# Gate logits of an attention and mixture-of-experts kernel: one pass per batch, added up in PSUM and turned on VectorE

## The chip, the cores and the metric

The kernel runs on one core of a Trainium2 chip. The metric is device time in microseconds of one execution, the median of several runs. The names of the engines are those of the profile: PE is TensorE's matmul, PEld its weight load, DVE is VectorE, ACT is ScalarE, POOL is GpSimd, SP is SyncE, whose queue carries most of the large transfers. SBUF is the on-chip memory, PSUM the eight banks of 512 float32 columns into which PE writes.

## What is computed

Eight batches of 448 tokens with 12 heads of 64 go through attention with a sigmoid in place of the softmax. The 768 values of each token then go through two gates and, by the larger logit, to one of 8 experts.

```python
scores = scale * np.matmul(q, k.transpose(0, 1, 3, 2)) - np.log(S)
attn_out = np.matmul(1.0 / (1.0 + np.exp(-scores)), v)
x = attn_out.transpose(0, 2, 1, 3).reshape(B * S, H * D)
logits = x @ w_gate                       # (3584, 8)
e_idx = np.argmax(logits, axis=1)
gate_w = softmax(logits)[np.arange(N), e_idx]
eom = 1.0 / (1.0 + np.exp(-(x @ w_output_gate)))
out[mask] = gate_w[mask, None] * eom[mask, e, None] * (np.maximum(x[mask] @ w1[e], 0.0) @ w2[e])
```

The last line runs for each expert e, with `mask = e_idx == e`.

## The kernel before

**Attention.** The 96 heads are 48 pairs, six pairs a batch. `attention` walks through 24 groups of two pairs in 7 units each, 168 units and two more, since the values run two units behind the scores. In each unit PE does four score matmuls (line 810) and four value matmuls (line 819), each of four in its own 64 by 64 corner of the array, and ACT one sigmoid over 896 columns (line 812). After units 3 and 6 of a group the function `evict` has DVE add the two halves of a pair's output from PSUM into an SBUF tile `x` (128 channels by 448 tokens, line 832), turn it in blocks of 32 (line 833) and, after a batch's last pair, has SP write the batch to DRAM as rows (line 835).

**Gates.** `wg` holds both gates' weights for each pair, 128 by 32, of which 16 columns are used. `gates(k)` runs in unit 3 of every second group, and once more after attention: four pairs' tiles `x` are multiplied with their weights at once, each pair in its own 32 columns of the array (line 849), so that each pair's part of the logits lands in its own 32 partitions of PSUM bank 6. DVE copies or adds these parts to a tile `gl` in SBUF (lines 856, 858, 859, 861). A batch has six pairs, so a call can end one batch and begin the next.

**Route.** `route(b)` is a generator in five pieces, one for each batch. The piece behind "logits" has PE turn `gl` in four chunks of 112 tokens (line 277, into bank 5, or bank 7 after attention), so that tokens lie on partitions; DVE adds the four 32-row parts (line 278) and finds the largest logit (lines 281 to 285, up to `oh`, a 0/1 mark). Behind "counts" PE counts marks with `tri` and `ones` (lines 293 to 299) and ACT takes sigmoids. Behind "places" ACT copies the counts and POOL works out each token's place in its expert's list (lines 303 to 313). Behind "rows" POOL writes each token's record into the lists in DRAM with four indirect DMAs (line 319). In attention the pieces run in units 5, 0, 1 and 3; the last batch's run in `side()` between steps of the first expert tile.

**Experts.** `slot(m)` takes 256 tokens of one expert. POOL gathers their rows (line 504), DVE turns them, ACT and DVE split rows and weights into a high and a low part (lines 538 to 545), PE does layer 1 (lines 582 and 583) and layer 2 (lines 607 to 609). Layer 1's sums go through three tiles that lie in the same memory as `gl`. The first slots take tokens of batches 0 to 5, so that the expert stage starts without the last batches.

**Order.** The program is recorded in the order in which it is written, engine by engine; no scheduler moves anything. Each engine runs its own instructions in that order.

## Time and profile before

| what | us |
|---|---|
| median of 3 runs (779.05 to 780.46) | 779.47 |
| the profiled execution, its own time | 779.45 |
| its span, first to last instruction | 777.74 |
| PE busy in the span | 765.6 |
| DVE busy | 498.2 |
| ACT busy | 488.1 |
| POOL busy | 354.6 |
| granted PE clock, share of full | 0.999 |

The span is what the rows below divide up; the 1.7 us between span and time lie around the program. Matmuls are pipelined: the length of one in a row includes its way through the array, so what one costs in a stream is read from the distance of starts. A float32 matmul stands in the trace as two records, each with a weight load of its own: line 849 has 48 matmuls and 96 records.

### The profile page before, as it was taken

The page shows a single profiled execution, that of the slowest core. Times are in us where ns is not written, and L with a number is a line of the kernel's source. Part 1 is how long each engine was busy: PE and PEld are TensorE (multiplying, and loading weights), DVE is VectorE, ACT ScalarE, POOL GpSimd, SP SyncE. Part 2 cuts the span into 40 slices and gives each one's busy share as a digit, 9 for nine tenths or more (in the row PEclk, how much of TensorE's full clock was granted, in tenths as well). Part 3 has the DMA queues.
Part 4 walks back from the last instruction along what each step waited for, and adds up shares of the span by engine and source line. Part 5 has one row for each costly group of instructions (what it writes and reads, how often), then busy time and mean ns, then how long its engine had stood idle before and what let it go on. Part 6 is the DMA issues. An engine that isn't in the chain of part 4 may idle for free. (4 is left out here: it accounts for less than half of the span.)

```text
span 777.7 us, 15123 instructions
## 1 busy us (share of the span) xinstructions
PE 765.6 (98%) x5724; PEld 559.8 (72%) x5724; DVE 498.2 (64%) x804; ACT 488.1 (63%) x662; POOL 354.6 (46%) x464
## 2 busy tenths in 40 slices
PE   9999999999999999999999999999999999999996
PEld 4333433333433369899999979999998999889785
DVE  3344444443455768977786577668576685977887
ACT  5666666666667757466574565657475574665686
POOL 4003301230331677778885676263462724524622
PEclk9999999999999999999999999999999999999999
DMA  7352544445258560147566487620146856387692
GB/s 262 136 214 98 190 161 174 165 144 214 72 215 297 180 202 16 42 152 257 214 239 244 164 309 265 223 72 31 51 150 220 300 174 214 124 329 252 227 409 65
DMA packets 37615, 145.20 MB, mean 187 GB/s; under 512 B 5639, under 2 KB 7791, under 8 KB 33552
## 3 DMA queue, kind: packets, MB, share of 16 engines
q1 hardware_dynamic: 27696, 119.56, 43.1%
q0 software_dynamic: 9824, 24.46, 9.4%
q8 instruction: 49, 0.80, 0.4%
q14 instruction: 46, 0.38, 0.1%
HBM read 152.61 MB, written 23.05 MB: 226 GB/s over the span
## 5 line engine op out<-in xcount | busy, mean ns | idle before, releaser
L812 ACT ACTIVATE a<-ps,bias_s 128x896 f32<-128x896 f32 x168 | 169.1, 1008 | 95.8 <-PE ps L810 95.8
L582 PE MATMUL ps<-rounded 128*128 128x512 f32 (+1 forms) x672 | 226.5, 386 | 1.3 <-PEq L1006 1.0
L504 POOL DMA_INDIRECT plain<-x_dram,lxs x122 | 182.1, 1493 | 65.2 <-issue 39.3
L583 PE MATMUL ps<-rounded 128*128 128x256 f32 (+1 forms) x672 | 184.1, 274 | 1.4 <-DVE due L617 1.2
L810 PE MATMUL ps<-kqv 64*64 64x448 f32 x1344 | 157.8, 540 | 0.4 <-ACT a L812 0.4
L819 PE MATMUL ps<-a,kqv 64*64 64x448 f32 x1344 | 156.6, 536 | 0.0
L607 PE MATMUL ps<-w2h,h 128*128 128x384 f32 x432 | 144.8, 335 | 0.0
L609 PE MATMUL ps<-w2h,h 128*128 128x384 f32 x432 | 144.4, 334 | 0.0
L608 PE MATMUL ps<-w2l,h 128*128 128x384 f32 x432 | 144.3, 334 | 0.0
L582 PEld LDWEIGHTS ps<-rounded 128*128 128x128 f32 x672 | 125.9, 187 | 25.4 <-issue 2.7
L539 DVE TENSOR_TENSOR w2l<-plain,w2h 128x1536 fp32r<-128x1536 f32 x60 | 105.2, 1757 | 58.7 <-ACT w2h L538 58.0
L583 PEld LDWEIGHTS ps<-rounded 128*128 128x128 f32 x672 | 127.2, 189 | 2.0 <-DVE rounded L545 2.0
L819 PEld LDWEIGHTS ps<-a,kqv 64*64 64x64 f32 x1344 | 51.6, 133 | 75.1 <-issue 74.2
L545 DVE TENSOR_TENSOR rounded<-plain,rounded 128x2048 fp32r<-128x2048 f32 x46 | 103.3, 2285 | 2.0 <-ACT rounded L542 2.0
L810 PEld LDWEIGHTS ps<-kqv 64*64 64x64 f32 x1344 | 48.6, 133 | 73.8 <-issue 60.4
L590 ACT COPY gl<-ps 128x256 f32<-128x256 f32 (+1 forms) x112 | 40.3, 360 | 93.2 <-PE ps L583 87.2
L538 ACT CAST w2h<-plain 128x1536 fp32r<-128x1536 f32 x60 | 88.2, 1473 | 16.2 <-PE ps L849 4.4
L542 ACT CAST rounded<-plain 128x2048 fp32r<-128x2048 f32 x46 | 87.3, 1903 | 0.0
L607 PEld LDWEIGHTS ps<-w2h,h 128*128 128x128 f32 x432 | 81.1, 188 | 2.3 <-issue 1.8
L608 PEld LDWEIGHTS ps<-w2l,h 128*128 128x128 f32 x432 | 81.1, 188 | 0.1
L609 PEld LDWEIGHTS ps<-w2h,h 128*128 128x128 f32 x432 | 81.1, 188 | 0.0
L303 POOL TENSOR_TENSOR pos<-pc,off 112x32 f32<-112x32 f32 x8 | 3.8, 474 | 146.2 <-ACT pc L301 146.2
(211 smaller groups left out, 728.7 us busy)
## 6 DMA issues: line engine op xcount, KB each, us to landing
plain<-w SPq DMA_DIRECT2D x68, 768.0 KB
plain<-w SPq DMA_DIRECT2D x48, 1024.0 KB
kqv<-kqv SPq DMA_DIRECT2D x23, 1344.0 KB
x_dram<-xt SPq DMA_DIRECT2D x8, 1344.0 KB
plain<-w SPq DMA_DIRECT2D x6, 512.0 KB
plain<-x_dram,lxs POOLq DMA_INDIRECT x122, 4.2
kqv<-kqv SPq DMA_DIRECT2D x1, 896.0 KB
lst<-plain POOLq DMA_DIRECT2D x1, 726.0 KB, 8.7
```

Source lines behind the costliest of these rows:

```text
L504: self.nc.gpsimd.indirect_dma_start(out=s["xg"][:, g], out_offset=None, in_=x4, in_offset=bass.IndirectOffsetOnAxis(ap=s["lx"][:, g:g + 1] ...
L538: self.nc.scalar.copy(hi, raw)
L539: self.nc.vector.tensor_tensor(lo, raw, r32(hi), ALU.subtract)
L545: self.nc.vector.tensor_tensor(self.w1p[1][k], self.w1r[:, 2 * k:2 * k + 2], r32(self.w1p[0][k]), ALU.subtract)
L582: nc.tensor.matmul(out, wh[d][:, c], both, start=(d == 0), stop=False)
L583: nc.tensor.matmul(ps[:, 0:n], wl[d][:, c], self.xc[:, d, 0, 0:n], start=False, stop=(d == 5))
L607: nc.tensor.matmul(ps, hh[:, f, tk], wh, start=(f == 0), stop=False)
L608: nc.tensor.matmul(ps, hh[:, f, tk], wl, start=False, stop=False)
L609: nc.tensor.matmul(ps, hl[:, f, tk], wh, start=False, stop=(f == 7))
L810: nc.tensor.matmul(ps[half[h], j, 0:S], kg[half[j], e, 0, o:o + 64], kg[half[j], e, 1], start=True, stop=True)
L812: nc.scalar.activation(at[u % 4], ps[:, :, 0:S], AF.Sigmoid, bias=self.bias_s, scale=1.0 / math.sqrt(D))
L819: nc.tensor.matmul(self.ps_o[e][h][half[j], 0:S], v[half[h], 6 if i == 3 else 3 * e + c, j], a[half[h], j], start=(i in ((0, 3 if h else 4 ...
```

## The change

`gates(b)` now runs once for each batch, in unit 3 of every third group and once after attention. All six pairs of a batch are kept in six tiles (two of them the tiles that were `gl`). Each pair's 448 tokens are cut into quarters of 128, 128, 128 and 64; the quarters take the four column groups of the array, and the six pairs add up in PSUM: 24 matmuls of 128 or 64 columns in one call where there were four of 448. The logits then stand in bank 6 whole, 32 rows for each quarter, and DVE turns them from PSUM into SBUF in blocks of 32 with two instructions (the fourth quarter has only two blocks). The copies and adds into `gl`, the four PE transposes and the sum over parts go away. Partitions now hold 128 tokens in two chunks and 96 in two, in place of four times 112; the constants, the marks and the scatter to the lists follow. The piece behind "logits" runs directly behind the gates. Batches 0, 2, 4 and 6 are routed a group earlier; only the "rows" of batch 6 stay where they were.

```diff
+        self.gp = ps[:, 6, 0:QT]
...
-        self.tok = cp.tile([CP, 2, NCH], I32, name="tok")
-        nc.gpsimd.iota(self.tok[:, 0], pattern=[[CP, NCH]], base=0, channel_multiplier=1)
-        nc.gpsimd.iota(self.meta[:, :, :, 4], pattern=[[S, B], [CP, NCH]], base=0, channel_multiplier=1,
-                       allow_small_or_imprecise_dtypes=True)
+        self.tok = cp.tile([128, 2, NCH], I32, name="tok")
+        for q in range(4):
+            r = slice(32 * q, 32 * q + 32)
+            nc.gpsimd.iota(self.tok[r, 0], pattern=[[32, NCH]], base=QT * q, channel_multiplier=1)
+            nc.gpsimd.iota(self.meta[r, :, :, 4], pattern=[[S, B], [32, NCH]], base=QT * q, channel_multiplier=1,
+                           allow_small_or_imprecise_dtypes=True)
...
+        self.spans = [(128, slice(0, 2)), (96, slice(2, 4))]
...
+        for n in ("lg", "oh"):
+            self.nc.gpsimd.memset(self.R[n], 0.0)
...
         yield "logits"
-        ps = self.mm_ps
-        for c in range(NCH):
-            nc.tensor.transpose(ps[0:CP, 128 * c:128 * c + 128], self.gl[b % 2][:, c * CP:(c + 1) * CP], self.ident)
-        v.tensor_reduce(R["lg"], ps[0:CP, 0:128 * NCH].rearrange("p (c e x) -> p c x e", c=NCH, e=4)[:, :, 0:16, :],
-                        AX.X, ALU.add)
+        for n, c in self.spans:
+            v.transpose(R["lg"][0:n, c].rearrange("p c x -> p (c x)"), self.gp[0:n, 32 * c.start:32 * c.stop])
...
-        v.tensor_tensor(R["oh"], R["rk"], bc(R["mf"][:, 1]), ALU.is_equal)
+        for n, c in self.spans:
+            v.tensor_tensor(R["oh"][0:n, c], R["rk"][0:n, c], bc(R["mf"][:, 1])[0:n, c], ALU.is_equal)
...
-        xts = [t(f"x{i}", [128, S]) for i in range(4)]
+        xts = self.gl + [t(f"x{i}", [128, S]) for i in range(4)]
...
-        def gates(k):
-            v, gp = nc.vector, self.ps_o[1][0]
-            for e in range(4):
-                nc.tensor.matmul(gp[32 * e:32 * e + 32, 0:S], self.wg[:, (4 * k + e) % NPAIR], xts[e],
-                                 start=True, stop=True)
-            for b in sorted({(4 * k + e) // NPAIR for e in range(4)}):
-                es = [e for e in range(4) if (4 * k + e) // NPAIR == b]
-                r = slice(32 * es[0], 32 * es[-1] + 32)
-                gl, src = self.gl[b % 2], gp[r, 0:S]
...
+        def gates(b):
+            for p in range(NPAIR):
+                for q in range(4):
+                    n = min(QT, S - QT * q)
+                    nc.tensor.matmul(self.gp[32 * q:32 * q + 32, 0:n], self.wg[:, p], xts[p][:, QT * q:QT * q + n],
+                                     start=(p == 0), stop=(p == NPAIR - 1))
+            routes.append(self.route(b))
+            want[0] = next(routes[0])
...
-            if i == 3 and g and g % 2 == 0:
-                gates(g // 2 - 1)
+            if i == 3 and g and g % 3 == 0:
+                gates(g // 3 - 1)
+                routing("logits")
...
-            for r, name in ((5, "logits"), (0, "counts"), (3, "rows")):
-                if i == r:
+            for r, name in ((0, "counts"), (3, "rows")):
+                if i == r and (name != "rows" or g != NG - 2):
                     routing(name)
         self.layer1_mm(0)
-        gates(NG // 2 - 1)
+        gates(B - 1)
```

**Where instructions stand.** In the program before, PE has around the second call of the gates and the first batch's transposes (names are output and input; `kqv` and `a` are attention's operands, `x` a pair's tile):

```order
L819 MATMUL ps<-a_145,kqv_142 64x448 x4
L849 MATMUL ps<-x_148,wg 32x448
L849 MATMUL ps<-x_149,wg 32x448
L849 MATMUL ps<-x_150,wg 32x448
L849 MATMUL ps<-x_151,wg 32x448
L810 MATMUL ps<-kqv_142 64x448 x4
L819 MATMUL ps<-a_146,kqv_142 64x448 x4
L810 MATMUL ps<-kqv_142 64x448 x4
L819 MATMUL ps<-a_147,kqv_142 64x448 x4
L277 MATMUL ps<-ident,gl_104 112x128 x4
L810 MATMUL ps<-kqv_142 64x448 x4
```

In the changed program, PE has for the whole of the first batch's logits (line 855 is the gates', `gl` now a pair's tile too):

```order
L855 MATMUL ps<-gl_110,wg 32x128 x3
L855 MATMUL ps<-gl_110,wg 32x64
L855 MATMUL ps<-gl_111,wg 32x128 x3
L855 MATMUL ps<-gl_111,wg 32x64
L855 MATMUL ps<-x_156,wg 32x128 x3
L855 MATMUL ps<-x_156,wg 32x64
L855 MATMUL ps<-x_157,wg 32x128 x3
L855 MATMUL ps<-x_157,wg 32x64
L855 MATMUL ps<-x_158,wg 32x128 x3
L855 MATMUL ps<-x_158,wg 32x64
L855 MATMUL ps<-x_159,wg 32x128 x3
L855 MATMUL ps<-x_159,wg 32x64
```

Two calls of four long matmuls and one set of transposes became one run of 24 short matmuls, behind a value matmul and ahead of a score matmul as before.

DVE, before, from the last call of the gates into the first expert slot (L539 are low parts of weights, L591 and L596 layer 1's sums and their low parts, L278 to L285 the last batch's logits):

```order
L858 TENSOR_TENSOR gl_105<-gl_105,ps 64x448
L859 COPY gl_105<-ps 64x448
L539 TENSOR_TENSOR w2l_2460<-plain,w2h 128x1536
L591 TENSOR_TENSOR gl_104<-gl_104,ps 128x256 x2
L596 SCALAR_TENSOR_TENSOR h_2458<-gl_104,h_2457 128x256
L539 TENSOR_TENSOR w2l_2460<-plain,w2h 128x1536
L278 TENSOR_REDUCE lg<-ps 112x64
L281 TENSOR_REDUCE mf<-lg 112x4
L282 TENSOR_TENSOR df<-lg,mf 112x32
L283 SCALAR_TENSOR_TENSOR rk<-df,rev 112x32
L284 TENSOR_REDUCE mf<-rk 112x4
L285 TENSOR_TENSOR oh<-rk,mf 112x32
```

The same place in the changed program (L544, L596 and L601 are the lines that were 539, 591 and 596):

```order
L544 TENSOR_TENSOR w2l_2578<-plain,w2h 128x1536
L596 TENSOR_TENSOR gl_110<-gl_110,ps 128x256 x2
L601 SCALAR_TENSOR_TENSOR h_2576<-gl_110,h_2575 128x256
L544 TENSOR_TENSOR w2l_2578<-plain,w2h 128x1536
L282 STREAM_TRANSPOSE lg<-ps 128x64
L282 STREAM_TRANSPOSE lg<-ps 96x64
L284 TENSOR_REDUCE mf<-lg 128x4
L285 TENSOR_TENSOR df<-lg,mf 128x32
L286 SCALAR_TENSOR_TENSOR rk<-df,rev 128x32
L287 TENSOR_REDUCE mf<-rk 128x4
L289 TENSOR_TENSOR oh<-rk,mf 128x16
L289 TENSOR_TENSOR oh<-rk,mf 96x16
```

The two passes over `gl` are gone from the front, two transposes stand where the sum stood, and the mark takes two instructions.

## Rows read from the trace of the kernel before

**Rows 1.** The page: the span, and busy time of each engine.
```profile
span 777.7 us, 15123 instructions
PE 765.6 (98%) x5724; PEld 559.8 (72%) x5724; DVE 498.2 (64%) x804; ACT 488.1 (63%) x662; POOL 354.6 (46%) x464
```

**Rows 2.** Busy time by stretch: from:to, length, each engine, clock, DMA.
```profile
5.00:278.00 273.00, 272.62 (x2855) 106.42 (x2857) 129.58 (x277) 178.44 (x205) 69.44 (x193) 1.00 0.51 181
278.00:745.00 467.00, 463.58 (x2718) 426.16 (x2714) 340.72 (x502) 284.23 (x427) 271.26 (x242) 1.00 0.54 188
```

**Rows 3.** Timeline of PE around one gates call: start, length, line, count.
```profile
50.50 0.93 PE L810 MATMUL ps<-kqv 64*64 64x448 f32 x8
...
52.00 0.93 PE L810 MATMUL ps<-kqv 64*64 64x448 f32 x8
...
53.61 0.96 PE L849 MATMUL ps<-x,wg 128*32 128x448 f32 x8
54.50 0.98 PE L810 MATMUL ps<-kqv 64*64 64x448 f32 x8
...
56.06 0.93 PE L810 MATMUL ps<-kqv 64*64 64x448 f32 x8
56.81 0.93 PE L819 MATMUL ps<-a,kqv 64*64 64x448 f32 x8
57.67 0.65 PE L277 MATMUL ps<-ident,gl 128*112 128x128 f32 x4
...
59.80 0.93 PE L810 MATMUL ps<-kqv 64*64 64x448 f32 x8
```

**Rows 4.** Line 849 alone: lengths in ns, least, median, most; a window in its first set.
```profile
L849 PE MATMUL ps<-x,wg x96: 539/551/563, 31.5 to 281.7; 128*32 128x448 f32 x96
...
31.52 0.58 PE L849 MATMUL ps<-x,wg 128*32 128x448 f32 x4
```

**Rows 5.** Line 277 alone: lengths in ns, and what ended idle time before it.
```profile
L277 PEld LDWEIGHTS ps<-ident,gl x32: 131/133/135, 57.7 to 284.6; 128*112 128x112 f32 x32
L277 PE MATMUL ps<-ident,gl x32: 272/273/323, 57.7 to 284.7; 128*112 128x128 f32 x32
...
  DVE xh L822: 4.2, 6
```

**Rows 6.** Timeline of PE: the last gates call, transposes and counts, in the first slot.
```profile
281.06 0.28 PE L583 MATMUL ps<-rounded 128*128 128x256 f32 x1
281.27 0.96 PE L849 MATMUL ps<-x,wg 128*32 128x448 f32 x8
282.16 0.50 PE L582 MATMUL ps<-rounded 128*128 128x512 f32 x1
...
284.24 0.28 PE L583 MATMUL ps<-rounded 128*128 128x256 f32 x1
284.36 0.60 PE L277 MATMUL ps<-ident,gl 128*112 128x128 f32 x4
284.71 0.48 PE L582 MATMUL ps<-rounded 128*128 128x512 f32 x1
...
291.15 0.19 PE L293 MATMUL ps<-oh,tri 112*128 112x32 bf16 x1
...
291.26 0.24 PE L299 MATMUL ps<-oh,ones 112*128 112x8 bf16 x4
```

**Rows 7.** Timeline of ACT and DVE at the same place.
```profile
282.34 1.48 ACT L538 CAST w2h<-plain 128x1536 fp32r<-128x1536 f32 x1 [4.43 <-PE ps L849]
...
287.81 1.76 DVE L539 TENSOR_TENSOR w2l<-plain,w2h 128x1536 fp32r<-128x1536 f32 x1 [0.95 <-ACT w2h L538]
289.49 0.42 DVE L278 TENSOR_REDUCE lg<-ps 112x64 f32<-112x256 f32 x1
...
290.90 0.19 DVE L285 TENSOR_TENSOR oh<-rk,mf 112x32 bf16<-112x32 f32 x1
```

**Rows 8.** Groups up to 345 us: busy us, mean ns; idle before, releaser.
```profile
L833 DVE STREAM_TRANSPOSE xt<-x 128x448 f32<-128x448 f32 x48 | 31.0, 645 | 1.6
L856 DVE COPY gl<-ps 128x448 f32<-128x448 f32 (+1 forms) x8 | 5.0, 626 | 7.8 <-PE ps L849 7.7
```

**Rows 9.** Timeline of PE late: the longest stall of the expert stage.
```profile
452.20 0.39 PE L583 MATMUL ps<-rounded 128*128 128x256 f32 x1 [1.24 <-DVE due L617]
```

More of the change, by code (lines that the diff above doesn't have):

```diff
@@ L26 @@
 NT = B * S
-CP = 112
-NCH = S // CP
+NCH = 4
+QT = 32 * NCH
 Q4 = DM // 4
@@ L106, in memory @@
         self.tmp_early = o + 4096
-        self.step = c(o + 8192, B, 4, dt=F32, parts=CP)
-        self.tokf = c(o + 8192 + 16 * B, NCH, 4, dt=F32, parts=CP)
+        self.step = c(o + 8192, B, 4, dt=F32)
+        self.tokf = c(o + 8192 + 16 * B, NCH, 4, dt=F32)
     def late_memory(self):
@@ L153, in constants @@
         nc.gpsimd.dma_start(self.wg[:, :, 0:16], self.wgo)
-        self.ones = cp.tile([CP, 128], BF16, name="ones")
+        self.ones = cp.tile([128, 128], BF16, name="ones")
         nc.gpsimd.memset(self.ones, 1.0)
-        self.tri = cp.tile([CP, 128], BF16, name="tri")
+        self.tri = cp.tile([128, 128], BF16, name="tri")
         nc.gpsimd.memset(self.tri, 1.0)
@@ L161, in constants @@
             t, pattern=pattern, base=base, channel_multiplier=0, allow_small_or_imprecise_dtypes=True)
-        self.rev = cp.tile([CP, E], F32, name="rev")
+        self.rev = cp.tile([128, E], F32, name="rev")
         iota(self.rev, [[-1, E]], E)
@@ L302, in route @@
         v.reciprocal(sg[:, 1], sg[:, 1])
-        tt(R["pos"], R["pc"][0:CP, 0:NCH * E].rearrange("p (c e) -> p c e", e=E),
-           self.off[0:CP].unsqueeze(1).broadcast_to([CP, NCH, E]), ALU.add)
+        tt(R["pos"], R["pc"][:, 0:NCH * E].rearrange("p (c e) -> p c e", e=E),
+           self.off.unsqueeze(1).broadcast_to([128, NCH, E]), ALU.add)
         tt(R["pos"], R["pos"], oh, ALU.mult)
@@ L318, in route @@
         for c in range(NCH):
+            n = self.spans[c // 2][0]
             g.indirect_dma_start(
-                out=self.lst, out_offset=bass.IndirectOffsetOnAxis(ap=R["posi"][:, c:c + 1], axis=0),
-                in_=meta[:, c, :], in_offset=None)
+                out=self.lst, out_offset=bass.IndirectOffsetOnAxis(ap=R["posi"][0:n, c:c + 1], axis=0),
+                in_=meta[0:n, c, :], in_offset=None)
             if b == B - 2:
@@ L830, in evict @@
             b, hp = divmod(m, NPAIR)
-            x, o = xts[m % 4], xt[b % 2]
+            x, o = xts[hp], xt[b % 2]
             nc.vector.tensor_tensor(x, xh, self.ps_o[m % 2][0][:, 0:S], ALU.add)
@@ L844, in routing @@
                     routes.pop(0)
-        def gates(k):
-            v, gp = nc.vector, self.ps_o[1][0]
-            for e in range(4):
-                nc.tensor.matmul(gp[32 * e:32 * e + 32, 0:S], self.wg[:, (4 * k + e) % NPAIR], xts[e],
-                                 start=True, stop=True)
-            for b in sorted({(4 * k + e) // NPAIR for e in range(4)}):
-                es = [e for e in range(4) if (4 * k + e) // NPAIR == b]
-                r = slice(32 * es[0], 32 * es[-1] + 32)
-                gl, src = self.gl[b % 2], gp[r, 0:S]
-                if b % 2 == 0 and k % 3 == 0 or b % 2 and k % 3 == 1:
-                    v.tensor_copy(gl[r], src)
-                elif b % 2 and k % 3 == 2:
-                    v.tensor_tensor(gl[64:128], gl[64:128], src[64:128], ALU.add)
-                    v.tensor_copy(gl[0:64], src[0:64])
-                else:
-                    v.tensor_tensor(gl[r], gl[r], src, ALU.add)
-            for e in range(4):
-                if (4 * k + e) % NPAIR == NPAIR - 1:
-                    routes.append(self.route((4 * k + e) // NPAIR))
-                    if len(routes) == 1:
-                        want[0] = next(routes[0])
+        def gates(b):
[6 more added lines that the diff above has]
+            want[0] = next(routes[0])
         warm = self.rounded[:, 0:256]
```

24 lines of the change are left out of this document (12 added, 12 removed).

## The prediction

> **What bounds the kernel now.** I read the page's busy shares first: PE is busy 98% of the span, no other engine above 64% [rows 1]. A mean over stages can hide a stage with another limit, so the stretches come next: in attention, 5 to 278 us, PE is busy 272.6 of 273.0 us, DVE 129.6, ACT 178.4 and POOL 69.4; in the expert stage up to 745 us PE is busy 463.6 of 467.0 [rows 2]. Busy is not yet "at its peak", so the third view is the timeline of PE. In a plain stretch score groups start at 50.50 and 52.00, one unit of 1.50 us with two groups of 0.75 [rows 3]. Anything that lengthens the distance between these starts is paid in full, since PE waits for nobody; anything that only makes DVE, ACT or POOL lighter is worth nothing in itself. So the sum below is one of PE time, and DVE enters only where PE waits for it.
>
> **What goes from PE in attention.** With a gates call between them, the score groups at 52.00 and 56.06 lie 4.06 us apart where two units take 3.00 [rows 3]: a call costs 1.06. Of this 0.75 is the call's columns (four matmuls side by side, as many columns as one group of attention); the other 0.31 is the entry into another shape of tile, the first weight load and the way back. Transposes cost 0.74: 56.06 to 59.80 is 3.74 [rows 3]. The table of waits says that the transposes waited for DVE's copy `xh`, 4.2 us over six times [rows 5]. I do not count that as a wait. The distance from the value group at 56.81 to the transposes at 57.67 is 0.86, 0.11 more than 0.75, and the way into the gates call costs about as much without such a wait. So no credit beyond 0.74 is due. Before, 11 calls and 7 sets of transposes lie in attention: 11 x 1.06 + 7 x 0.74 = 16.8 us.
>
> **What comes to PE.** Seven calls in attention, each with 24 matmuls of which every one is two records: 12 sets of four, each set as long as its longest, 128 columns. The switch is the same 0.31. What does a set cost? The old call shows that four column groups run at once: four records start within a window in which one takes 563 ns and all four take 0.58 us [rows 4]. No row has sets of 128 columns in this shape. The nearest is the transposes, 128 float32 columns each with a weight load of its own: four in the first slot take 0.60 us, one takes 0.273, so starts lie (0.60 - 0.27) / 3 = 0.11 apart [rows 5, 6], although each load is recorded as 131 to 135 ns. Their loads, of 112 columns, hide under the matmul before; the new ones have four times 32, so I take 0.11. Bound below: a set can hardly cost less than its share of the columns, 0.75 / 2 / 448 x 128 = 0.107. Bound above: each set pays the weight load that the first set of an old call shows, 563 - 539 = 24 ns [rows 4], so 0.134. A call is then 0.31 + 12 x 0.11 = 1.63 (1.59 to 1.92), seven are 11.4. Attention gains 16.8 - 11.4 = **5.4 us**.
>
> Here a rule of the Trainium skill speaks against the change. "TensorE: Matmul & The Clock Gate", section "Part 3: Packing small matmuls", says that a weight load overlaps running matmuls only where its row group differs; all four quarters use all rows. By that rule the upper bound holds, attention gains 3.3 us and the time would come out near 777.1. The rows speak the other way: in the old call only one set shows the 24 ns and the other is at 539 [rows 4].
>
> **DVE in attention.** It loses the passes over `gl`, 626 ns for a typical one [rows 8], and the sum over parts, and gets two transposes from PSUM. No row has these: 128 x 448 takes 645 ns [rows 8], so between that and nothing; by length I take about 0.25 each, as long together as the 0.42 of the sum [rows 7]. All this lies beside PE. The new chain starts right behind the gates and takes about 2 us; behind it on DVE is the copy `xh` of the next unit, some 0.4 us late. Its PSUM bank is written again four units (6 us) later, so PE does not see it; the counts come four units later too. If that cover were gone, 0.4 us a batch, 3 us in all, would come back. POOL's steps of even batches, and four scatters of 128 or 96 rows for 112, lie in its idle time: 69.4 of 273 us busy [rows 2]. In the last third of attention POOL also issues the gathers of the first slots; the places of batch 6 now stand behind the first gathers and ahead of the lists of slots 1 and 2, which are needed only some 10 us later, with its scatters. Constants on POOL get a few more instructions at the start, long before the first use. I put these at nothing.
>
> **The end of attention.** The last gates call is in the path of the expert stage. Its way in and out costs what it did, its sets 12 x 0.11 = 1.32 for 0.75: **+0.57**. The transposes there cost 284.71 - 284.36 = 0.35, no more, since the tile's shape does not change [rows 6]. They go, but I give no credit. The counts start at 291.15, and the marks they need are written by DVE from 290.90 for 0.19, thus at 291.09 [rows 6, 7]: only 0.06 us of slack. That DVE chain hangs on ACT's split at 282.34, which waits for the gates' last matmul [rows 7], and from there on splits and low parts in turn, not on the transposes. PE without transposes arrives 0.35 earlier and waits 0.3; and two transposes and a second instruction for the mark make the chain some 0.15 longer. So this place is **+0.15**, and the end +0.7 in all. The late stages are as before; their longest stall, 1.24 us, is local to one slot [rows 9].
>
> **Sum.** -5.4 + 0.7 = -4.7 us. The profiled execution took 779.45 (span 777.74), the median is 779.47: they agree, so **774.8**.
>
> **The rivals.**
> - *Exposed weight loads.* 12 x 0.024 x 8 calls = 2.3 us more: 777.1. For it: the shape has never been run in sets this short, with four loads within 0.11 us. Against it: the second set at 539, the transposes at 0.11.
> - *The quarters do not run side by side* (the slower end). Place: the 12 sets of each call. If short passes go one by one, a set costs 3 x 0.11 + 0.055 = 0.385, a call 0.31 + 4.62 = 4.9, eight calls 8 x 3.3 = 26 us more: about 801. It decides from the point at which the eight calls take up the 4.7 us: a set of 0.11 + 4.7 / 96 = 0.16 us. Against it: four long passes in 0.58 [rows 4]; and PE issues four records of 8 columns, each with a weight load, in 0.24 us [rows 6], of which the last takes 0.17, so some 25 ns apart and four in 0.10, just under 0.11. For it: 48 pairs of load and matmul in a row is longer than any such run in the trace.
> - The same page of the Trainium skill, section "Back-to-back issue gap", gives about 81 ns for each load and matmul of 128 columns in a stream; by it 48 pairs would be 3.9 us, a call 4.2, and the kernel near 795, which lies within the one-by-one case and has its chance there. The four matmuls in 0.58 us [rows 4] speak against it for column groups.
> - *The expert stage shifts.* POOL's list work for batch 6 ends earlier, the transposes are off PE, and the stalls behind row groups such as the 1.24 us [rows 9] may fall otherwise: 1 us either way, 773.8 or 775.8. That the change does not do what it says I exclude: the order shows the copies and transposes gone.
>
> **How the numbers follow.** My forecast, 774.8 with its own spread of 1 us for the expert stage, gets 0.74; exposed loads (777.1) 0.13; the one-by-one case, with anything between 0.16 and 0.385 us a set, 0.06; a larger shift of the expert stage, half of it to either side, 0.07. The range reaches from 773.5, a little under the lower bound of a set (8 x 0.04 less) with a microsecond from the expert stage, to 777.3, which takes in the exposed loads. About 0.2% of 779.5, 1.6 us, is what a measurement of this kernel can tell from no change; so faster means below 777.9, slower above 781.0. Faster: nearly all of the first two cases and half of the last, 0.89. Same: 0.05. Slower: 0.06.
>
> **What would show it.** In the new trace, PE around a gates call: score groups 1.63 us further apart than 3.00, the call's 48 records within about 1.5 us, and no PE transposes. A call of 1.9 says exposed loads; of over 2.3, that quarters queue up. Attention should end 5.4 us earlier. In the first slot PE should stand for some 0.4 us ahead of the counts, waiting for the mark. The prediction is wrong if PE waits in attention for DVE's chain, or if the expert stage from the counts on is longer or shorter than before by more than 1 us.

## The result

The changed kernel takes **772.56 us** (median of 6 runs, 771.59 to 774.66), the kernel before beside it 779.73: a ratio of 0.9898, 95% interval 0.9882 to 0.9914. The forecast was 774.8 with a range down to 773.5. The sign is right, and so is what the gates are worth in attention; the gain is 7.2 us where 4.7 were forecast, and the time lies 0.9 us under the range. In one sitting (a set of runs taken together) the times of the kernel before spread by 1.4 to 6.0 us, and its median was 779.7 to 780.8 in five sittings and 786.2 in the last. So ratios are taken within a sitting, and terms under 1 us are read from traces, not from times.

The page of the changed kernel, against [rows 1]:

```profile
span 770.5 us, 15647 instructions
PE 759.4 (99%) x5980; PEld 566.5 (74%) x5980; DVE 486.4 (63%) x800; ACT 488.7 (63%) x662; POOL 350.2 (45%) x472
```

The busy times by stretch, with the columns of [rows 2]; attention now ends at 273.9 us:

```profile
5.85:273.90 268.05, 267.66 (x3081) 111.88 (x3080) 119.23 (x273) 178.60 (x205) 70.47 (x199) 1.00 0.52 185
287.00:745.00 458.00, 456.17 (x2670) 423.44 (x2671) 338.02 (x492) 286.54 (x428) 256.86 (x233) 1.00 0.55 193
```

PE is as full in attention as before; it simply has less to do. The 7.25 us between the two spans, cut at starts of PE's instructions:

| stretch of PE | before, us | after, us | difference |
|---|---|---|---|
| to the first score group | 5.19 | 5.85 | +0.66 |
| attention, to the first layer-1 matmul | 273.77 | 268.07 | -5.70 |
| from there to the counts | 12.19 | 12.72 | +0.53 |
| the fourth and the sixth expert tile, in which PE stalled | 33.74 + 35.49 | 33.28 + 33.28 | -2.67 |
| all the rest | 417.36 | 417.29 | -0.07 |

The first line, and 0.39 us more within the second, are a late start of PE in this run and no part of the change (fourth question): the 18th unit of attention starts at 29.90 us before and at 30.95 after. With equal starts attention would have gained 6.09 us, and the spans would lie 8.3 us apart.

**The gates.** PE's timeline around the first call, to be held against [rows 3]:

```profile
41.47 0.93 PE L815 MATMUL ps<-kqv 64*64 64x448 f32 x8
...
43.09 0.53 PE L855 MATMUL ps<-gl,wg 128*32 128x128 f32 x13
...
43.55 1.05 PE L855 MATMUL ps<-x,wg 128*32 128x128 f32 x30
44.53 0.98 PE L815 MATMUL ps<-kqv 64*64 64x448 f32 x8
...
46.08 0.93 PE L815 MATMUL ps<-kqv 64*64 64x448 f32 x8
```

The score groups at 41.47 and 46.08 lie two units apart, 4.61 us where two units take 3.00 [rows 3]: a call costs 1.61, forecast 1.63. The records start in twelve sets of four. From the first set to the second it is 0.134 us in every call, from there on 0.109 to 0.110 from set to set. No PE transposes are left.

**The first slot**, against [rows 6, 7]; PE and then DVE:

```profile
276.20 0.53 PE L855 MATMUL ps<-gl,wg 128*32 128x128 f32 x13
...
277.64 0.50 PE L587 MATMUL ps<-rounded 128*128 128x512 f32 x1
...
286.10 0.28 PE L588 MATMUL ps<-rounded 128*128 128x256 f32 x1
286.64 0.18 PE L297 MATMUL ps<-oh,tri 128*128 128x32 bf16 x1 [0.25 <-DVE oh L289]
```

```profile
284.96 0.37 DVE L282 STREAM_TRANSPOSE lg<-ps 128x64 f32<-128x64 f32 x2
...
286.32 0.26 DVE L289 TENSOR_TENSOR oh<-rk,mf 128x16 bf16<-128x16 f32 x2
```

The last call takes 1.44 (276.20 to 277.64) for 0.89 (281.27 to 282.16 [rows 6]): +0.55. From 286.10 to the counts 0.54 us pass where one short matmul takes 0.12: PE waits 0.42 us for the mark, which DVE ends at 286.58.

**The expert stage** is where most of the difference to the forecast lies. PE's table of waits from 300 to 640 us, before and then after (who waited for whom, total us, times, longest):

```profile
PE ps L583 <- DVE due L617: 1.2, 1, 1.2
PE ps L582 <- DVE gl L591: 0.3, 1, 0.3
```

```profile
PE ps L587 <- DVE gl L596: 0.3, 1, 0.3
```

The stall of [rows 9] is gone, with smaller ones around it: the sixth expert tile took 35.49 us on PE (448.77 to 484.26) and now takes 33.28, like the plain tiles around it; the fourth lost 0.46.

### The profile page after: what moved, and what is told of

It is laid out like the page before. It is cut to its first block, busy times and chain, and to the rows that moved or that the text cites. A ratio compares the mean times of both kernels' runs of the same rounds, so it can differ in the third digit from the quotient of the medians.

```text
span 770.5 us, 15647 instructions
## 1 busy us (share of the span) xinstructions
PE 759.4 (99%) x5980; PEld 566.5 (74%) x5980; DVE 486.4 (63%) x800; ACT 488.7 (63%) x662; POOL 350.2 (45%) x472
## 5 line engine op out<-in xcount | busy, mean ns | idle before, releaser
L509 POOL DMA_INDIRECT plain<-x_dram,lxs x122 | 180.2, 1477 | 64.8 <-issue 32.5
L544 DVE TENSOR_TENSOR w2l<-plain,w2h 128x1536 fp32r<-128x1536 f32 x60 | 105.2, 1757 | 66.5 <-ACT w2h L543 61.3
L634 POOL DMA_INDIRECT out<-y,due x11 | 18.2, 1658 | 112.4 <-ACT gl L595 91.7
```

The costliest lines, as they stand in the source:

```text
L509: self.nc.gpsimd.indirect_dma_start(out=s["xg"][:, g], out_offset=None, in_=x4, in_offset=bass.IndirectOffsetOnAxis(ap=s["lx"][:, g:g + 1] ...
L544: self.nc.vector.tensor_tensor(lo, raw, r32(hi), ALU.subtract)
```

## The experiments

**First question: is it attention, and does PE decide?** `after_transposes` puts the PE transposes back beside the new gates, seven sets, two units behind each call.

```diff
+            if i == 5 and g and g % 3 == 0:
+                for c in range(4):
+                    nc.tensor.transpose(self.mm_ps[0:112, 128 * c:128 * c + 128], self.ident[:, 0:112], self.ident)
```

> The changed kernel with four PE transposes of a constant into bank 5 put back in unit 5 of every group that has gates in attention, seven sets, their result unused. Theory 1 (attention's part is a sum of PE time): 7 x 0.74 = 5.2 us more, 777.8. Rival (part of what transposes cost before was their wait for DVE's copy, or PE is not what bounds attention in the changed kernel): 1 to 3 us more.

Measured: 777.79 (776.82 to 779.21), ratio 0.9959 [0.9944, 0.9974]; from its 18th unit to the first layer-1 matmul attention takes 248.15 us for 242.97, which is 5.18 longer, 7 x 0.74. The work is extra, its result unused. So PE time in attention is paid one for one, transposes cost 0.74 as read from [rows 3], and the expert stage stays without stall: the transposes have no part in it.

`after_quarters` exchanges the two loops of a gates call.

```diff
-            for p in range(NPAIR):
-                for q in range(4):
+            for q in range(4):
+                for p in range(NPAIR):
```

> The changed kernel with the two loops of a gates call exchanged: all six pairs of one token quarter, then the next quarter, the same 24 matmuls. If four column groups run side by side only where their instructions follow one another, each matmul now stands alone: a call is 12 x 0.385 = 4.6 us of columns for 1.29, 3.3 us more, eight calls 26 us, about 799; that is the price that the prediction put on quarters that queue up. If the order does not matter: 772.6.

Measured: 787.93 (787.85 to 788.87), ratio 1.0093 [1.0066, 1.0120]. A call's records start over 3.35 us instead of 1.24; that is 2.1 us more a call, not 3.3. PE's timeline of one call shows why:

```profile
42.58 0.62 PE L855 MATMUL ps<-gl,wg 128*32 128x128 f32 x4
43.04 0.71 PE L855 MATMUL ps<-x,wg 128*32 128x128 f32 x5
43.48 0.30 PE L855 MATMUL ps<-gl,wg 128*32 128x128 f32 x1
43.58 0.27 PE L855 MATMUL ps<-x,wg 128*32 128x128 f32 x1
43.61 0.27 PE L855 MATMUL ps<-gl,wg 128*32 128x128 f32 x1
...
46.08 0.98 PE L815 MATMUL ps<-kqv 64*64 64x448 f32 x8
```

Inside a quarter a record takes 0.11 us alone, as long as four of them in four quarters together. Where one quarter ends and the next begins (43.48 on) the last four records of the one and the first four of the next run at once, which the forecast's price of a queue left out. So here column groups run side by side only when their instructions stand next to one another: the order of the two loops is worth 15 us, and the rival "the quarters do not run side by side" names a real price, in the wrong loop order.

**Second question: where do 2.67 us of the expert stage go?** The first theory: POOL's work on the lists of the later tiles. In the kernel before the gather of the sixth tile starts at 426.56, 11.07 us behind the start of the fifth tile's layer 1 at 415.49; after, at 418.95, 8.43 us behind 410.52. DVE's turn of the sixth tile waits 7.1 us for it, after 4.9, and PE waits for the DVE work behind that turn. `before_defer` moves POOL's last list copies in the kernel before out of the gather's way.

```diff
-            for _ in range(4):
+            for _ in range(14):
                 yield
             self.spread_lists(self.lr[5], *at(20, 4))
```

> The kernel before, with POOL's last list copies (two spreads of 32 rows and the copies for the wide slots) moved from ahead of the gather for the sixth expert tile to behind it; nothing in attention changes. Theory 1 (some 2.6 us of the 7.2 us came from a PE stall of the expert stage that the list work on POOL causes by making that gather late): the stall of 2.2 us at the start of the sixth tile goes, 779.6 becomes about 777.2 (776.6 to 777.8). Rival (all of the 7.2 us lies in attention and the stall has nothing to do with POOL's list work): 779.6, within 0.6.

Measured: 783.2 (779.92 to 788.05), ratio 1.0033 [1.0003, 1.0062]: a miss. DVE's turn waited only 3.1 us, but the copies now stood ahead of the scatter of `y`, and ACT waited for that scatter:

```profile
ACT y L627 <- DMA out<-y,due: 10.7, 1, 10.7
```

The stall moved and grew: the sixth tile took 40.69 us. Not all of this is waiting. PE stood for 4.8 us, and while it stood the granted clock fell to its lower level, for 6.8 us (the figure 0.50):

```profile
458.60:465.40 6.80, 5.08 (x16) 4.31 (x17) 5.28 (x9) 3.29 (x8) 3.16 (x2) 0.50 0.66 209
```

The same edit in the changed kernel, `after_defer`:

> The changed kernel with the same move of POOL's last list copies. Theory 1: the gather is early enough there already in most executions, so 772.4, 0 to 0.4 us below the changed kernel, with no execution near 774.7. Rival: no difference in either respect.

Measured: 773.9 (771.48 to 775.68), ratio 0.9910 [0.9880, 0.9939]; no stall in its trace, and the spread of times did not go: inconclusive. Two further runs change when the list loads are issued. `after_poollate` holds them up by seven idle memsets in the changed kernel; `before_rowsfirst` lets them pass the first slot's second `out` scatter in the kernel before (`later` issues it).

```diff
+            for _ in range(7):
+                self.nc.gpsimd.memset(self.meta, 0.0)
             self.load_rows(0)
```

> The changed kernel with about 3 us of extra POOL work (seven writes of zeros to a tile that is no longer used) ahead of the list loads in the second expert tile; no other engine's work changes. Theory 1 (POOL's lead of some 4 us in the list work is what keeps the gather for the sixth tile early): the PE stall comes back, 772.6 becomes 774.6 to 775.4. Rival (the stall is away for another reason): 772.6, within 0.5.

Measured: 774.39 (773.05 to 776.86), ratio 0.9911 [0.9884, 0.9939]; both stalls are back in the trace, +0.47 in the fourth and +1.97 in the sixth tile, with the wait of before. The times alone could not show it, since after_defer, without a stall, has 773.9 in the same sitting.

```profile
PE ps L588 <- DVE due L622: 1.2, 1, 1.2
```

The edit of `before_rowsfirst`, without the lines that make `later`:

```diff
...
             for i in (1, 3):
                 self.load_rows(i)
                 self.load_rows(i + 1)
+                if i == 3:
+                    self.later()
                 yield
...
```

> The kernel before, with one thing moved on POOL: the second `out` scatter of the first slot, which waits some 3 us for the first one to land, now stands behind the five list loads instead of ahead of them. Nothing of attention or of the gates is touched. Theory 1 (the 2.65 us that the expert stage loses in the kernel before are POOL's list loads, caught behind that scatter until DVE's long run begins): the stalls of 0.45 and 2.2 us go, PE's stretch of 18.84 us in the sixth expert tile becomes 16.64, and the time is 2.65 us under the kernel before, some 777. Rival (the stalls belong to the old gates or to DVE's turn itself): no change, 779.5.

Measured: 778.16 (777.24 to 780.17), ratio 0.9968 [0.9956, 0.9981]; in the trace both tiles take 33.28. So the 2.67 us hang on the place of POOL's list loads, and have nothing to do with attention's work. The same move in the changed kernel, run twice, the second time beside the changed kernel itself:

> The same move in the changed kernel. Theory 1: no stall is left there that it could take away, so 772.5 again, within 0.5 us, and a ratio to the kernel before of 0.990 to 0.992. Rival (the list loads are late in both kernels, by less in the changed one): another 0.5 us or more less, 772.0 or under.

> The changed kernel once more, beside the next one. 772.5, ratio 0.989 to 0.991. If the later start of the changed kernel (first score group at 5.85 us for 5.19) belongs to the kernel, it is at 5.8 or 5.9 again; if it is chance, it can lie anywhere from 5.2.

> The changed kernel with the second `out` scatter of the first slot behind the list loads, once more, beside the changed kernel on the same chip. If the list loads are at times late in the changed kernel too, its runs near 774 and above go: all runs within 771.8 to 772.5, a median 0.3 to 0.6 us under the changed kernel. Otherwise both have the same median and the same runs above 774.

Measured: 772.07, then 772.21 beside 772.01 for the unmoved kernel, ratios 0.9883 [0.9856, 0.9910], 0.9899 [0.9883, 0.9916] and 0.9897 [0.9881, 0.9914]. The three agree: no stall is left there to take away, and this is no better version.

**Third question: why are the list loads earlier after the change?** POOL's DMA instructions at the end of the first slot, before and after (`out<-y` are the two scatters, `hb<-lst` the list loads):

```profile
329.71 1.11 POOL L629 DMA_INDIRECT out<-y,lts  x1 [0.30 <-issue]
334.25 1.15 POOL L629 DMA_INDIRECT out<-y,lts  x1 [3.43 <-ACT h L595]
335.70 0.91 POOL L493 DMA_INDIRECT hb<-lst,gl  x1 [0.30 <-issue]
...
338.11 9.57 POOL L493 DMA_INDIRECT hb<-lst,gl  x1 [0.30 <-issue]
```

```profile
325.20 1.13 POOL L634 DMA_INDIRECT out<-y,lts  x1 [0.30 <-issue]
329.18 1.06 POOL L634 DMA_INDIRECT out<-y,lts  x1 [2.85 <-issue]
330.54 0.91 POOL L498 DMA_INDIRECT hb<-lst,gl  x1 [0.30 <-issue]
...
334.11 8.42 POOL L498 DMA_INDIRECT hb<-lst,gl  x1 [0.30 <-issue]
```

Before, the second scatter starts 3.43 us behind the end of the first (3.47 in before_defer); in every run of the changed kernel that keeps this order it is 2.85 to 2.87. And a load that takes 0.9 us alone takes 8 to 10 once DVE's run of three long tensor operations has begun. The first guess was POOL's own program: the change adds eight constants there. `before_pad8` adds eight such instructions to the kernel before, `after_unpad` takes the eight off POOL in the changed kernel.

```diff
+        for _ in range(3):
+            nc.gpsimd.iota(self.tok[:, 0], pattern=[[CP, NCH]], base=0, channel_multiplier=1)
+            nc.gpsimd.iota(self.meta[:, :, :, 4], pattern=[[S, B], [CP, NCH]], base=0, channel_multiplier=1,
+                           allow_small_or_imprecise_dtypes=True)
+        for _ in range(2):
+            nc.gpsimd.memset(self.run, 0.0)
```

> The kernel before with eight small POOL instructions more among the constants at the start (six iotas and two memsets repeated, results unchanged), as many as the change adds there. Nothing else differs. In the kernel before the second `out` scatter of the first slot stands 3.43 us after the first (3.47 in before_defer), in every run of the changed kernel 2.85 to 2.87, and before shows one short transfer of instructions during that wait that the changed kernel does not. Theory (where POOL's instruction stream is fetched depends on how many instructions came before; the added constants moved a fetch out of that wait): the wait is 2.85, three list loads instead of two stand ahead of DVE's long run, the stalls of 0.46 and 2.21 us are gone, and the time is 2.67 us under the kernel before, some 777 (ratio 0.9965). Rival (the wait depends on the gates, the transposes or the data on its way): 3.43, the stalls stay, 779.5 to 780.4.

> The changed kernel with its eight additional POOL instructions among the constants taken off POOL again (the iotas of a quarter are one iota and three adds on DVE, the two memsets are on DVE), so that POOL has as many instructions ahead as in the kernel before. Theory: the wait ahead of the second `out` scatter is 3.4 us again, two list loads stand ahead of DVE's long run, the stalls of 0.46 and 2.2 us come back, and the time is 2.67 us over the changed kernel, some 775. Rival: 2.85, no stalls, 772 to 772.5.

Measured: before_pad8 780.66, ratio 0.9994 [0.9971, 1.0017], the second scatter 3.54 us behind the first, both stalls there. It had three list loads ahead of the long one, like the changed kernel, so that count, which the theory had named as the cause, is not it. after_unpad 780.80, ratio 0.9995 [0.9977, 1.0013], the wait 2.86 and no stall. Its time says nothing on the question: the adds on DVE came ahead of the memset for which PE's first matmul waits, and PE came to its first score group 7.7 us later than in the changed kernel (780.80 less 7.7 is 773.1):

```profile
PE ps L867 <- DVE rounded L863: 9.0, 1, 9.0
```

Both verdicts on the stall are against the guess. What is left is what lies in the wait itself. In the kernel before the DMA view of 331.9 to 332.6 us shows, among the scatter's rows, one transfer of instructions (queue, kind: packets, MB, share):

```profile
q0 software_dynamic: 42, 0.17, 61.2%
q14 instruction: 1, 0.01, 2.8%
```

It comes 1.3 us behind the end of the scatter's instruction, and the scatter's last row lands at 2.17 us instead of 1.70. In every run of the changed kernel it comes 2.2 to 2.6 us ahead of the end of that instruction, and the last row lands at 1.70 or 1.71. Counting ACT's instructions in the traces, it comes in both kernels when ACT has had 448. The changed kernel has seven more on ACT by then, waits at the copies `pc`, one a batch (line 305; line 301 before has none). `before_act7` adds seven small activations at the very start, where ACT is idle; `before_act7_pad8` has these and the eight on POOL.

```diff
-        nc.scalar.activation(self.off[:, 0:1], self.bias_s, AF.Sigmoid)
+        for _ in range(8):
+            nc.scalar.activation(self.off[:, 0:1], self.bias_s, AF.Sigmoid)
```

> The kernel before with seven small ACT instructions more at its very start (one activation of 128x1 repeated), where ACT has nothing else to do. The traces show one short transfer of instructions that comes when ACT is at its 448th instruction, in both kernels; the changed kernel has seven more waits on ACT ahead of that place (one a batch, at the copy `pc`), so there it comes 2.3 us ahead of the first slot's first `out` scatter's end, and in the kernel before 1.3 us behind it, among the scatter's rows, whose last ends at 2.2 us instead of 1.7. Theory (this transfer makes the second scatter, the list loads and all that follows on POOL late): with ACT seven instructions ahead the transfer comes at -2.3, the wait ahead of the second scatter is 2.85 for 3.43, the list loads end 0.6 us earlier or more, and the stalls of 0.46 and 2.21 us go: 2.67 us under the kernel before, some 777 (ratio 0.9965). If 0.6 us is not enough by itself: the wait is 2.85, and the stalls get smaller by some 0.6. Rival (the transfer is not ACT's, or has no part in it): 3.43, the stalls stay.

> Both: the seven ACT instructions and the eight POOL constants of before_pad8, so that both engines have as many instructions ahead of the expert stage as in the changed kernel. Theory: everything on POOL lies as in the changed kernel, the wait is 2.85, three list loads stand ahead of DVE's long run, the stalls are gone, some 777 (ratio 0.9965). If the two pads together do not take the stalls away, the cause lies in the gates or in the routing's own order after all, and the place of the instructions is not it.

Measured, in a sitting in which the kernel before takes 786.16: 783.04 (781.77 to 784.91), ratio 0.9954 [0.9933, 0.9975]; and 783.10, ratio 0.9958 [0.9939, 0.9977]. POOL in before_act7:

```profile
336.93 1.11 POOL L630 DMA_INDIRECT out<-y,lts  x1 [0.31 <-issue]
340.88 1.07 POOL L630 DMA_INDIRECT out<-y,lts  x1 [2.84 <-issue]
...
344.66 0.87 POOL L494 DMA_INDIRECT hb<-lst,gl  x1 [0.30 <-issue]
345.84 8.51 POOL L494 DMA_INDIRECT hb<-lst,gl  x1 [0.30 <-issue]
```

The transfer lies 2.36 us ahead, the wait is 2.84, the sixth tile's gather starts 8.44 us behind the start of the fifth tile (430.74 after 422.30), and the fourth and sixth tile take 33.28 and 33.31 us (33.28 and 33.57 with the eight on POOL; where 0.29 us come from is open). Seven idle instructions on ACT, in a kernel otherwise unchanged, bring what the change brought beside its purpose.

Two things limit this. The kernel before has no trace from that sitting: that it stalled there too is taken from the times, 3.1 us by medians. And both traces of that sitting have another wait of PE, 5 to 6 us in two to four units near the end of attention, which no other trace shows and whose cause is open; in before_act7 the granted clock is 0.50 behind it, from 266.7 to 270.1 us. It is over before the first slot: there the first scatter ends 51.89 us behind the first layer-1 matmul, 51.86 in the kernel before.

How 0.6 us become 2.67 can be followed from tile to tile. Each tile's rows are gathered by POOL and then turned by DVE, whose long run of three operations comes behind the turn. Places are in us behind the start of the tile on PE; the delay in after_poollate is that of its memsets:

| run | wait ahead of the second scatter | list loads end, tile 2 | fourth tile's last gather, tile 3 | DVE's turn waits for it | DVE's long run begins, tile 3 | sixth tile's gather, tile 5 |
|---|---|---|---|---|---|---|
| before | 3.43 | 35.44 | 20.08 | 4.85 | 27.76 | 11.07 |
| before_pad8 | 3.54 | 34.28 | 18.82 | 4.91 | 27.83 | 11.06 |
| after_poollate | 2.85 | 36.20 | 20.07 | 4.89 | 27.81 | 10.94 |
| after | 2.85 | 33.59 | 14.66 | 0 | 22.80 | 8.43 |
| before_act7 | 2.84 | 33.73 | 14.66 | 0 | 22.80 | 8.44 |

POOL's loads, copies and gathers get longer where they fall beside DVE's operations, so a delay of 0.7 us at the end of the list loads (before_pad8) is over 4 us at the fourth tile's last gather. DVE then has to wait for these rows, its long run begins 5 us later, and the fourth tile stalls. The later run covers other copies of POOL, and so the delay goes on to the sixth tile. POOL before at the end of its lists:

```profile
406.54 2.17 POOL L464 CAST lxs<-wg 32x32 int32<-32x32 f32 x1
408.65 2.25 POOL L466 CAST lts<-wg 32x8 int32<-32x8 f32 x1
410.86 2.25 POOL L467 COPY lts<-wg 32x8 f32<-32x8 f32 x1
...
426.56 2.23 POOL L504 DMA_INDIRECT plain<-x_dram,lxs  x1 [8.03 <-issue]
```

the same after,

```profile
400.94 2.18 POOL L469 CAST gl<-lt 32x32 int32<-32x32 f32 x1
403.06 2.25 POOL L471 CAST gl<-lt 32x8 int32<-32x8 f32 x1
405.27 2.25 POOL L472 COPY gl<-lt 32x8 f32<-32x8 f32 x1
...
418.95 1.04 POOL L509 DMA_INDIRECT plain<-x_dram,lxs  x1 [8.03 <-DVE w2l L544]
```

and DVE meanwhile, before (after, the same from 400.77):

```profile
406.36 6.69 DVE L545 TENSOR_TENSOR rounded<-plain,rounded 128x2048 fp32r<-128x2048 f32 x3
```

A copy of 0.2 us takes 2.2 beside that run, as long as each of its three operations (6.69 / 3 = 2.23); beside the 128x512 operations just ahead, 0.64 us each, copies take 0.65. A copy that starts beside such an operation ends with it, so POOL does three in the run, however many it has left. After, these three (`gl<-lt`) are the last of the lists' copies and only eight short instructions follow, the last of them in 1.77 us beside DVE's next long operation; before, POOL comes to the run with twelve copies fewer done, and does these behind it, one of them in 1.71 us. The 8.03 us ahead of the gather, at a `drain` on POOL, are the same in both. The Trainium skill, "GPSIMD Engine Reference", section "Specifications", says that GpSimd shares its SBUF interfaces with VectorE and contends with instructions of two SBUF inputs; the rows agree, and give the price here: the rest of VectorE's operation.

**Fourth question: the rest of attention.** In the kernel before one value group near the end of attention takes 1.33 us for 0.93. PE, DVE and SP's queue:

```profile
270.02 1.33 PE L819 MATMUL ps<-a,kqv 64*64 64x448 f32 x8
```

```profile
267.80 1.78 DVE L564 STREAM_TRANSPOSE plain<-plain 128x1536 f32<-128x1536 f32 x1 [1.27 <-DMA plain<-x_dram,lxs]
```

```profile
262.99 7.04 SPq L525 DMA_DIRECT2D plain<-w  x2
```

The first tile's last gather is issued at 263.45, behind a weight load that goes out at 262.99; the turn waits 1.27 us for its rows, ACT for the turn, PE for ACT's sigmoid: 0.56 us by the distances of starts. In the changed kernel the load goes out at 259.70, behind the gather's last issue at 258.70, and no one waits there. `before_rows_load` sends that load one unit later, behind DVE's turn, on top of before_rowsfirst (whose lines are left out).

```diff
...
         for k in range(4):
-            if u == -9 + 2 * k:
+            if u == -9 + 2 * k and k:
...
         if u == -8:
             self.turn_x(s)
+            self.nc.vector.memset(self.w2r[0:1, 0, 0:1], 0.0)
+            self.load_w(s, self.w2, self.w2r, [0])
```

> The kernel before with the second `out` scatter behind the list loads, as in before_rowsfirst, and one thing more: the first weight load of w2, which goes out nine units from the end of attention, is issued one unit later, behind DVE's turn of the first tile. Theory: in the kernel before this load goes out at 262.99 us while the last gather of the first tile is still to be issued (263.45 to 264.40), and holds its rows up; the turn waits 1.3 to 1.6 us for them, ACT waits for the turn, and PE stalls 0.55 us in one unit. Then the wait of the turn goes, attention gets 0.5 us shorter than the 274.05 us of before_rowsfirst, and the time is 0.5 us under its 777.3 to 778.2. Rival (the rows are late in themselves, whatever else is on its way): the turn still waits over 1 us and nothing changes.

Measured: 778.92 (777.06 to 781.35), ratio 0.9984 [0.9971, 0.9998], no better than before_rowsfirst; but its attention is 273.32 us for 274.05, the load goes out at 269.33, the turn no longer waits for rows, and the value group is whole:

```profile
270.81 0.93 PE L823 MATMUL ps<-a,kqv 64*64 64x448 f32 x8
```

The trace bears the theory out; the median does not show it. In the profiled run PE began attention at 5.87 us for 5.24, which takes most of the gain away again; whether that is so in the other runs is not known.

That late start is the first line of the table above. It is no matter of the change: it also stood in kernels before (5.87 in before_rows_load and before_act7), and the changed kernels had 5.42 to 5.86. Its form is seen in the first row, the 20 matmuls that stand ahead of attention, before and after:

```profile
1.30 3.96 PE L873 MATMUL ps<-rounded 128*128 128x256 f32 x20 [1.30 <-DVE rounded L869]
```

```profile
1.29 4.64 PE L865 MATMUL ps<-rounded 128*128 128x256 f32 x20 [1.29 <-DVE rounded L861]
```

After, all but the first start 0.213 us apart; before, the first 14 do, and the last five 0.11 to 0.12. At 256 columns each, 0.213 us is 1.2 GHz, the lower of the clock's two levels. The table by stretch gives a granted clock of 1.00 there in both, but the traces hold no record of the clock for that time. The first record, at the upper level, begins at 4.30 us before, just where the starts draw together, and at 6.67 us after, when PE is already in attention. Over sixteen traces it begins between 4.21 and 7.43 us, and the 18th unit of attention starts between 29.87 and 31.34 us in the same order, 0.45 us later for each us (after_unpad, whose PE starts late, has 14.48). The same kernel has 6.67 in one run and 5.44 in after_again, whose first score group comes at 5.70: this is a matter of the run, and what sets the moment stays open. From the 18th unit to the first layer-1 matmul the changed kernel takes 242.97 us in every trace in which its gates are as they were and no transposes are added; the kernel before takes 249.06, and before_rows_load 248.50.

**Fifth question: the first slot.** `after_countslate` has the counts and places one step later, so that the mark is there.

```diff
             yield
             yield
+            yield
             next(rt)
             yield
             next(rt)
-            yield
             yield
             for _ in rt:
```

> The changed kernel, with the routing steps for the last batch's counts and places each one step of the first slot later, so that DVE's mark is written before PE comes to the counts. If the 0.53 us on PE ahead of the counts is the wait for that mark: the gap at the counts goes from 0.53 to about 0.1, the first slot from 13.05 to about 12.6, the time from 772.6 to about 772.2. Rival (the wait covers another one, so that PE stands as long one step later, or POOL's lists fall behind): 772.6 or more; if the lists fall behind as in the run with late POOL work, some 774.5.

Measured: 772.34 (771.42 to 774.49), ratio 0.9896 [0.9865, 0.9927]. PE no longer stands at the counts, but at the next layer-1 group instead:

```profile
286.18 0.50 PE L587 MATMUL ps<-rounded 128*128 128x512 f32 x1 [0.58 <-DVE gl L596]
```

From the first layer-1 matmul to the start of the third tile it is 70.15 us, in the changed kernel 70.04. The rival holds: DVE as a whole is behind PE there, by the logits chain it has to do, and which instruction of PE meets it first does not matter.

## Right and wrong, step by step

**Attention.** Forecast -5.4. A call costs 1.60 to 1.61 for 1.63, a set 0.109 to 0.110 for 0.11 (the first of a call 0.134), a set of transposes 0.74 as read. Seven new calls and what went give -5.53 (248.50 to 242.97); the stall of two units that went on its own gives another -0.56; 0.39 came back in the first 17 units of that run, which began at the lower speed. Together -5.70. The mechanism and the sizes of the gates hold. The 0.56 is a term that the forecast put at nothing: it took it that PE waits for nobody in attention, and the table of PE's waits does show none there, since the wait lies hidden in a value group that takes 1.33 us for 0.93 (fourth question). That the late start took back 1.05 us in all is luck of the profiled runs, and it hides a part of how far the forecast was off.

**Exposed weight loads.** Forecast as a rival at 777.1; did not happen. The 24 ns of [rows 4] come back once a call, in the first set (0.134 for 0.109), as in the old call; the other sets are not longer than their columns. The Trainium skill, "TensorE: Matmul & The Clock Gate", section "Part 3: Packing small matmuls", says from traces that a load overlaps running matmuls only where its row group differs; here all loads use all rows, four of them per 0.109 us, and nothing of them shows behind the first set. The trace disagrees with that sentence. It does fit what the same section says of the mechanism, that a load into the background weight buffer is pulled ahead as well.

**One by one.** Did not happen, since the pairs' loop is outside. after_quarters shows that the price is real in the other order, 2.1 us a call for the 3.3 of the forecast, whose term left out that neighbouring quarters overlap at their seams.

**DVE in attention at nothing.** Right: no wait of PE on DVE's chain; the two transposes take 0.37 for the 0.5 estimated.

**The first slot.** +0.7 forecast, +0.53 measured. The last call +0.55 for +0.57; the transposes -0.35; the wait for the mark +0.42 for some 0.4; -0.09 lies in the matmuls between. The refusal of a credit for the transposes was right, and after_countslate shows that it is a matter of DVE, not of the counts' place.

**The expert stage "as before".** This is the step that failed. It said that the late stages stay as they are and that the longest stall, 1.24 us, is local to one slot [rows 9], and so it put the expert stage at nothing. The stall is the visible end of a chain through POOL's lists, gather and DVE's turn, worth 2.67 us. The chain hung on 0.6 us at a scatter some 120 us earlier, and these on the place of one transfer of ACT's instructions. Without these 2.67 us the time would be some 775.2, inside the range. The forecast's own sign of being wrong, an expert stage changed by more than 1 us, was met. The rival "expert stage shifts" had the right place with 1 us for 2.67, and the wrong cause (earlier list work of batch 6, transposes off PE); a larger shift to this side had half of 0.07. That ACT's stream grows by seven waits could not be read from the order of instructions, which lists none.

**Left open.** What the change is worth with neither kernel stalling in the expert stage follows from the moved versions: 778.16 and 772.07, or 6.1 us by medians, 5.2 by the profiled runs (777.29 and 772.13), of whose starts 1.2 us differ. Why the kernel before spreads by 1.4 to 6.0 us in a sitting and the changed one by 0.9 to 3.1 is not settled; the start is worth up to 1.5 us of it in the traces. That the place of ACT's instructions decides the stall was shown in one direction only: no run moved the transfer back into the scatter in the changed kernel. What puts the transfer at ACT's 448th instruction was not varied either.

## What to carry to other kernels

Count a stall that ends on PE back to its first cause before calling it local: where a queue's short work can fall beside another engine's long run, half a microsecond decides microseconds, and any edit, even one of a few waits on an engine that limits nothing, can move it. So compare the stages that the change does not touch, and test a gain found there with a pad that does nothing. Small matmuls in column groups cost here no more than their columns (0.109 us a set for 0.107) and a fixed 0.3 us a call, if the loop over the groups is the inner one. And hold the first microseconds of two traces against each other before their spans are compared.

## What the runs showed of the hardware

- Four column groups of 128 float32 columns, each with a load of 128x32, follow one another at 0.109 to 0.110 us behind the first set (0.134), though each load is recorded at 106 to 110 ns; in the other loop order a single group takes as long as four.
- A transfer of one block of instructions among a scatter's rows made its last row land 0.5 us later, and POOL's next scatter 0.6 us later. This is so in all three traces with these scatters in their old order in which the transfer falls there (before, before_defer, before_pad8), and in none in which it does not.
- POOL's 32x8 copies take 0.18 us alone; beside DVE's operations of two inputs they end with the operation, 0.65 us beside 128x512 and 2.25 beside 128x2048. POOL's indirect loads take 0.87 us alone and 8.4 to 9.6 beside a run of these.
- PE's first matmuls start 0.213 us apart until the first record of the granted clock, which begins between 4.21 and 7.43 us from run to run; a stretch without a record reads 1.00 in the table by stretch.
- The granted clock fell to 0.50 within a wait of PE of 4.8 us in before_defer, for 6.8 us.
